# Attending two pairs of heads in one step, with both denominators in one PSUM bank and normalisation apart

## The chip, the cores and the metric

The kernel runs on one core of one Trainium2 chip. The metric is the device time of one execution in microseconds (us), as the median of the runs shown; smaller is better. The core has five engines that work side by side, each on a queue of its own that it takes in order: TensorE (PE in the profile, its weight loads PEld), VectorE (DVE), ScalarE (ACT), GpSimd (POOL) and SyncE (SP), which here only issues transfers. Matmul results stand in banks of PSUM, from which ACT and DVE move them on.

## What is computed

Three stages: linear attention with exponential features, a gated feed-forward network with an RMS norm, and a soft mixture of experts. The changed lines belong to the first stage, the features and the attention of the queries; the second stage is what runs around them.

```python
def phi(x):                                   # q, k, v: 4 x 8 heads x 576 x 64; w_phi: 64 x 128
    proj = einsum('bhsd,df->bhsf', x, w_phi)
    proj = proj - max(abs(proj), axis=-1)
    return concatenate([exp(proj), exp(-proj)], axis=-1)
q_p, k_p = phi(q), phi(k)
kv, z = einsum('bhsf,bhsd->bhfd', k_p, v), sum(k_p, axis=2)
x = einsum('bhsf,bhfd->bhsd', q_p, kv) / (einsum('bhsf,bhf->bhs', q_p, z) + 1e-6)
x = x as 2304 tokens x 512                    # then:
xn = x / sqrt(mean(x*x) + 1e-6) * rms_g
x = (silu(xn @ w_gate) * (xn @ w_val)) @ w_out          # 512 -> 1536 -> 512
return soft_moe(x)                            # 8 experts, 4 slots each, w1 and w2 per expert
```

## The kernel before

The 2304 tokens are worked in six blocks of 384. A first phase computes the features of the keys and kv for the four batches, converts the weights of the feed-forward network, and does the queries of block 0. Then the feed-forward network runs block by block, and in the background of block 0 the queries of block 1, in that of blocks 1 to 4 the queries of blocks 2 to 5 are prepared (class Reduced, the one that the change touches). Behind block 5 the experts run, for which 32 weight transfers of 1 MB are issued from block 5 on.

In a block, m runs over 12 slices of 128 hidden features. For each slice the loop writes gate(m + 1) (12 matmuls into pg, then tanh on ACT at L801 and a product on DVE at L802), value (12 matmuls into pv, a product on DVE at L806), and the output of slice m (9 matmuls into three acc banks); then t is split into hh (ACT, L102) and hl (DVE, L105), which the output matmuls of the next round read. Below, pg(m), pv(m) and acc(m) are these groups of matmuls for slice m; pg(0') is that of the next block. The products are made from high and low parts, so the inputs of a block are split too: for m = 11, split_block makes xnh0 to xnh3 (ACT) and xnl0 to xnl3 (DVE) out of xraw, the prepared queries of the next block. Each pg and pv reads them in the order xnh0, xnh0, xnl0, xnh1, and so on.

After gate, after value and after output, fill() inserts background steps: 36 slots in a block, numbered 0 to 35, slot 3m behind gate(m + 1), 3m + 1 behind its value, 3m + 2 behind the output of m. The table REDUCED says at which slot each step of the queries runs, the table PSLOTS the nine steps of post, the work on the previous block's result: three transposes at 1, 4 and 7, logits (matmuls LT) at 12, rows at 14, dturn at 16, dispatch (sps, which reads d) at 18, combine at 20, cturn (transposes ctp) at 24. The steps of the queries of one block, for 8 heads h in 4 pairs c, are:

- feature(h), L271: two matmuls into qP, a copy on ACT, an all-reduce of the largest value on POOL (L280); at slots 0, 2, 4, 8, 9, 14, 15, 20
- exps(h), L282: a subtraction on DVE and two exponentials on ACT; at slots 3, 5, 7, 11, 12, 17, 18, 23
- attend(c), L197: matmuls num (L206) and den (L214), the copy of num to xraw (ACT, L216), 1e-6 added to den (DVE, L218), reciprocal (DVE, L219), eight copies of 32 x 192 that spread it over the partitions (ACT, L224), the product with xraw (DVE, L225), a square (ACT) and the sum of squares s (DVE, L232); at slots 6, 12, 18, 24
- scale, L238: matmuls ssq over s, an inverse root in eleven steps on DVE for three values a partition, its spread to dg (DVE, L246), an all-reduce on POOL (L293); at slot 27
- out, L251: four scalings of xraw on DVE (L254); at slot 30

PSUM: three banks acc, two banks gv for pg and pv in turn, three banks misc for everything in the background. The features of a head lie in a tile e, of which there are three. The compiler's scheduler can move instructions of an engine by a few places against the order in which they are written, so that the order shown below is the one after it.

Of the kernel before, what the change touches and what calls it, by code (L numbers as in the profile page):

```python
# [7 lines left out]
F32 = mybir.dt.float32  # L8
F32R = mybir.dt.float32r
U32 = mybir.dt.uint32  # L10
AF = mybir.ActivationFunctionType
ALU = mybir.AluOpType
# [4 lines left out]
NB, NH, SEQ, HD, DF = 4, 8, 576, 64, 128  # L17
NT, DM, DFF = 2304, 512, 1536
# [3 lines left out]
BLK = 384  # L22
# [6 lines left out]
KCONV, MCONV = (3, 2), (2, 1)  # L29
# [6 lines left out]
REDUCED = [0, 0, 2, 3, 5, 6, 4, 8, 7, 11, 12, 9, 14, 12, 17, 18, 15, 20, 18, 23, 24, 27, 30]  # L36
# [28 lines left out]
def tile_kernel(ctx: ExitStack, tc: tile.TileContext, q2T, qT, kT, v, wbd, wg, wv, wo, rmsg, phi, w1, w2, consts, out):  # L65
# [107 lines left out]
    kvt = {}  # L173
# [82 lines left out]
    class Reduced(Q):  # L256
# [14 lines left out]
        def feature(self, h):  # L271
            x = self.x.pop(h)
            self.split(h + 1)
            self.load(h + 4)
            p = self.psum("qP", [128, BLK])
            PE.matmul(out=p, lhsT=ws, rhs=x, start=True, stop=False)
            PE.matmul(out=p, lhsT=wl, rhs=x, start=False, stop=True)
            e = self.e[h] = self.sp.tile([128, 2, BLK], F32, tag="e", name="qe", bufs=3)
            ACT.copy(out=e[:, 1], in_=p)  # L279
            POOL.partition_all_reduce(e[:, 0], e[:, 1], channels=128, reduce_op=bass_isa.ReduceOp.absmax)  # L280
# [6 lines left out]

        def spare(self):
            e = self.sp.tile([128, 2, BLK], F32, tag="e", name="dg", bufs=3)
            return e[:, 0], e[:, 1]  # L290
# [9 lines left out]
        def steps(self):  # L300
            def first():
                self.split(0)
                self.load(3)

            f = [lambda h=h: self.feature(h) for h in range(NH)]
            a = [lambda c=c: self.attend(c) for c in range(4)]
            g = [lambda h=h: self.exps(h) for h in range(NH)]
            s = [first, *(x for c in range(4) for x in (f[2 * c], f[2 * c + 1], g[2 * c], g[2 * c + 1], a[c])), self.scale, self.out]
            return sorted(zip(REDUCED, s), key=lambda x: x[0])

# [291 lines left out]
    Z_run = stp.tile([96, 1], F32, name="Z_run")  # L602
    with ExitStack() as p2:
# [228 lines left out]
        for _ in range(2):  # L832
            conv_load(sp, MCONV, sp, stp)
        for blk in range(NBLK):
            acc = [ps.tile([128, DM], F32, tag=f"acc{i}", name=f"acc{i}", bufs=1) for i in range(TPB)]
            qsteps, qnext = qnext or [], None
            if blk == 1:
# [7 lines left out]
                S_run = stp.tile([128, 2 * DM], F32, tag="S", name="S_run", bufs=1)[0:96, 0:DM]  # L845
# [21 lines left out]
            def fill():  # L867
                done[0] += 1
                if blk == 0:
# [6 lines left out]
                    if n == 2:  # L876
                        conv_load(sp, MCONV, sp, stp)
# [183 lines left out]
```

## Time and profile before

| what | us |
|---|---|
| median of 3 runs | 748.27 (746.10 to 750.22) |
| the profiled execution, its own time | 745.82 |
| its span, first to last instruction | 743.8 |
| TensorE busy in the span | 714.6 (96%) |
| DVE, ACT, POOL busy | 428.1, 371.2, 108.3 |

The span is what the trace covers; the time of an execution lies some 2 us above it. An engine counts as busy while one of its instructions runs; matmuls are pipelined, so their lengths in a timeline overlap, and the distance from one start to the next is what one costs. Behind a timeline row stands, in brackets, how long the engine was idle before it and which instruction it waited for. Idle time of an engine costs only if the bound engine waits for it.

### The profile page before, as it was taken

What the parts mean: (1) busy time and instruction counts of PE and PEld (TensorE: products, weight loads), DVE (VectorE), ACT (ScalarE), POOL (GpSimd) and SP (SyncE); (2) the same over time, 40 slices, a digit from 0 to 9 for tenths busy, and PEclk for the clock granted to TensorE, in tenths of its full rate; (3) what the DMA queues carried; (4) which work ended last, traced back from release to release, by engine and by line L of the source; (5) the groups of instructions that cost most, each with busy time, mean ns of one, the idle gap of its engine ahead of it and who ended that gap; (6) DMA issues with size and microseconds to landing.
All of it is one profiled execution on the core that took longest, in us unless ns stands there. A gap on an engine that the chain in (4) does not pass through costs nothing.

```text
span 743.8 us, 12360 instructions
## 1 busy us (share of the span) xinstructions
PE 714.6 (96%) x4919; PEld 576.0 (77%) x4919; DVE 428.1 (58%) x808; ACT 371.2 (50%) x805; POOL 108.3 (15%) x60
## 2 busy tenths in 40 slices
PE   6999898999899999999999999999999999999994
PEld 4555554888789888898888988889888899988343
DVE  5888956688746557555575565655556453332413
ACT  6789854688644465344653446533465331212102
POOL 0222210134200112011120121101211010000100
PEclk9999999999999999999999999999999999999997
DMA  9674211545010100101000010000100046567898
GB/s 321 231 251 171 72 44 45 200 158 200 1 61 22 33 22 22 48 0 33 22 23 20 1 33 22 23 19 0 33 1 2 9 170 248 204 227 291 292 385 312
DMA packets 25145, 79.45 MB, mean 107 GB/s; under 512 B 2688, under 2 KB 13376, under 8 KB 18688
## 3 DMA queue, kind: packets, MB, share of 16 engines
q1 hardware_dynamic: 24864, 77.79, 29.6%
q10 hardware_dynamic: 224, 0.88, 0.4%
q8 instruction: 38, 0.62, 0.4%
q14 instruction: 19, 0.16, 0.1%
HBM read 71.99 MB, written 6.67 MB: 106 GB/s over the span
## 4 chain that ended last, share of the span: by engine, by line
PE 73%; ACT 10%; DVE 6%; DMA 5%; issue 2%; POOL 1%; SPq 0%; ACTq 0%; DVEq 0%; POOLq 0%
PE pv L794 18%; PE pg L794 17%; PE acc L819 6%; PE acc L820 6%; PE acc L821 6%; PE num L206 4%; PE kacc L439 3%; DMA eu<-in_w_dram 2%; PE den L214 2%; ACT e L224 2%; PE kacc L448 2%; DVE wt L137 1%; DMA wraw<-in_wg_dram 1%; ACT wt L127 1%; PE P L394 1%
## 5 line engine op out<-in xcount | busy, mean ns | idle before, releaser
L794 PE MATMUL pv<-xnh,wv 128*128 128x384 f32 x576 | 151.5, 344 | 0.0
L794 PE MATMUL pg<-xnh,wg 128*128 128x384 f32 x576 | 150.2, 342 | 1.2 <-DVE t L802 1.0
L794 PEld LDWEIGHTS pg<-xnh,wg 128*128 128x128 f32 x576 | 104.7, 188 | 7.2 <-DVE t L802 1.5
L794 PEld LDWEIGHTS pv<-xnh,wv 128*128 128x128 f32 x576 | 103.1, 188 | 7.0 <-issue 6.7
L794 PE MATMUL pv<-xnl,wv 128*128 128x384 f32 x288 | 97.7, 339 | 0.0
L794 PE MATMUL pg<-xnl,wg 128*128 128x384 f32 x288 | 97.5, 338 | 0.0
L819 PE MATMUL acc<-wo,hh 128*128 128x512 f32 x216 | 88.5, 410 | 0.4 <-ACT hh L102 0.4
L280 POOL PARTITION_ALL_REDUCE qe<-qe x32 | 50.0, 1561 | 262.7 <-ACT qe L279 243.0
L820 PE MATMUL acc<-wo,hh 128*128 128x512 f32 x216 | 85.8, 397 | 0.0
L821 PE MATMUL acc<-wo,hl 128*128 128x512 f32 x216 | 85.3, 395 | 0.0
L102 ACT CAST hh<-t 128x384 fp32r<-128x384 f32 x72 | 36.7, 510 | 80.9 <-PE acc L820 69.8
L105 DVE TENSOR_TENSOR hl<-t,hh 128x384 fp32r<-128x384 f32 x72 | 41.3, 574 | 53.7 <-ACT hh L102 51.2
L802 DVE SCALAR_TENSOR_TENSOR t<-t,pg 128x384 f32<-128x384 f32 x72 | 39.7, 551 | 51.7 <-ACT t L801 51.6
L801 ACT ACTIVATE t<-pg 128x384 f32<-128x384 f32 x72 | 35.1, 488 | 62.8 <-PE pg L794 62.8
L224 ACT COPY qe<-qe 32x192 f32<-32x192 f32 x128 | 44.8, 350 | 31.7 <-DVE qe L219 30.4
L806 DVE TENSOR_TENSOR t<-t,pv 128x384 f32<-128x384 f32 x72 | 39.7, 552 | 30.3 <-PE pv L794 29.0
L794 PEld LDWEIGHTS pg<-xnl,wg 128*128 128x128 f32 x288 | 54.0, 188 | 0.3 <-DVE xnl L105 0.3
L794 PEld LDWEIGHTS pv<-xnl,wv 128*128 128x128 f32 x288 | 54.1, 188 | 0.1
L439 PE MATMUL kacc<-kp,vt 128*64 128x256 f32 (+1 forms) x320 | 43.9, 399 | 5.4 <-ACT kp L416 5.3
L821 PEld LDWEIGHTS acc<-wo,hl 128*128 128x128 f32 x216 | 40.6, 188 | 9.8
L819 PEld LDWEIGHTS acc<-wo,hh 128*128 128x128 f32 x216 | 40.7, 189 | 8.1 <-ACT hh L102 0.9
L820 PEld LDWEIGHTS acc<-wo,hh 128*128 128x128 f32 x216 | 40.7, 188 | 6.5
(187 smaller groups left out, 1069.3 us busy)
## 6 DMA issues: line engine op xcount, KB each, us to landing
eu<-in_w_dram SPq DMA_DIRECT2D x32, 1024.0 KB, 6.0
wraw<-in_wg_dram SPq DMA_DIRECT2D x6, 1024.0 KB, 5.3
wraw<-in_wv_dram SPq DMA_DIRECT2D x6, 1024.0 KB, 6.5
wraw<-in_wo_dram SPq DMA_DIRECT2D x6, 1024.0 KB, 6.2
qraw<-in_qT_dram SPq DMA_DIRECT2D x32, 192.0 KB, 2.3
raw<-in_kT_dram SPq DMA_DIRECT2D x18, 256.0 KB, 3.7
vt<-in_v_dram SPq DMA_DIRECT2D x18, 256.0 KB, 2.9
out_dram<-ob SPq DMA_DIRECT2D x18, 256.0 KB, 3.4
```

What stands on the lines that cost most here:

```text
L102: ACT.copy(out=hi, in_=src)
L105: (lo_eng or POOL).tensor_tensor(out=lo, in0=src, in1=hi.bitcast(F32), op=ALU.subtract)
L224: ACT.copy(out=rd[64 * hh + 32 * r:64 * hh + 32 * r + 32, g], in_=dn[o:o + 32])
L280: POOL.partition_all_reduce(e[:, 0], e[:, 1], channels=128, reduce_op=bass_isa.ReduceOp.absmax)
L439: PE.matmul(out=kva[o0:o0 + 64, hh // 2], lhsT=self.vt[r0:r1, h], rhs=kp[r0:r1, hh].rearrange("p s f -> p (s f)"), start=first and hh < 2, ...
L794: PE.matmul(out=p, lhsT=w[:, a, c], rhs=x, start=n == 0, stop=n == 11)
L801: ACT.activation(out=t, in_=g, func=AF.Tanh, scale=0.5)
L802: DVE.scalar_tensor_tensor(out=t, in0=t, scalar=1.0, in1=g, op0=ALU.add, op1=ALU.mult)
L806: DVE.tensor_tensor(out=t, in0=t, in1=wide("v", m, xs), op=ALU.mult)
L819: PE.matmul(out=acc[i], lhsT=hh[:, s], rhs=w[:, 0], start=m == 0, stop=False)
L820: PE.matmul(out=acc[i], lhsT=hh[:, s], rhs=w[:, 1], start=False, stop=False)
L821: PE.matmul(out=acc[i], lhsT=hl[:, s], rhs=w[:, 0], start=False, stop=m == MF - 1)
```

## The change

In place of attend(c) at four slots there are two steps attend2(c0), for pairs 0 and 1 at slot 12 and for pairs 2 and 3 at slot 24. Each takes num of the first pair, num of the second, then den of both, in two halves of one misc bank; so it holds all three misc banks where attend(c) held two. The evictions of num and the additions of 1e-6 belong to it. The rest, from the reciprocal to the sum of squares, is a step normalise(c) for each pair, at slots 13, 14, 25 and 26. Features and exponentials keep their slots. scale moves from 27 to 29, out from 30 to 31. Since features now wait longer for their attend, there are five tiles e. To make room, S_run (the running result of dispatch) gets a tile of its own, and the second buffer of the weight conversion in block 0 moves to the pool of the first.

```diff
--- before.py
+++ after.py
@@ -26,14 +26,14 @@
 NJ = MF // 2
 NPRE = 9
 LOW = 0.93 * 2.0 ** -29
-KCONV, MCONV = (3, 2), (2, 1)
+KCONV, MCONV = (3, 2), (2, 2)
 NX = 3
 NLEFT = 2
 ELEFT = 4
 CTURN = 4
 CEVERY = 3
 PSLOTS = [1, 4, 7, 12, 14, 16, 18, 20, 24]
-REDUCED = [0, 0, 2, 3, 5, 6, 4, 8, 7, 11, 12, 9, 14, 12, 17, 18, 15, 20, 18, 23, 24, 27, 30]
+REDUCED = [0, 0, 2, 4, 8, 9, 14, 15, 20, 3, 5, 7, 11, 12, 17, 18, 23, 12, 24, 13, 14, 25, 26, 29, 31]
 TURNED0 = [2, 8, 14, 20, 12, 15, 20, 26, 28, 31]
 TURNED1 = [0, 7, 14, 21, 6, 13, 20, 26, 28, 30]
 
@@ -275,7 +275,7 @@
             p = self.psum("qP", [128, BLK])
             PE.matmul(out=p, lhsT=ws, rhs=x, start=True, stop=False)
             PE.matmul(out=p, lhsT=wl, rhs=x, start=False, stop=True)
-            e = self.e[h] = self.sp.tile([128, 2, BLK], F32, tag="e", name="qe", bufs=3)
+            e = self.e[h] = self.sp.tile([128, 2, BLK], F32, tag="e", name="qe", bufs=5)
             ACT.copy(out=e[:, 1], in_=p)
             POOL.partition_all_reduce(e[:, 0], e[:, 1], channels=128, reduce_op=bass_isa.ReduceOp.absmax)
 
@@ -285,8 +285,57 @@
             ACT.activation(out=e[:, 0], in_=e[:, 1], func=AF.Exp)
             ACT.activation(out=e[:, 1], in_=e[:, 1], func=AF.Exp, scale=-1.0)
 
+        def attend2(self, c0):
+
+            if c0 == 0:
+                xraw[self.blk] = xp.tile([128, 4, BLK], F32, tag="xraw", name="xraw", bufs=1)
+            cs = c0, c0 + 1
+            nums = {c: self.psum("num", [128, BLK]) for c in cs}
+            for c in cs:
+                for b, t0, t1 in block_parts(self.blk):
+                    for s in range(2):
+                        for hh in range(2):
+                            PE.matmul(out=nums[c][64 * hh:64 * hh + 64, t0:t1], lhsT=kvt[b][:, 2 * c + hh, s, 0:HD],
+                                      rhs=self.e[2 * c + hh][:, s, t0:t1], start=s == 0, stop=s == 1, skip_group_check=True)
+            den = self.psum("den", [128, 2, BLK // 2])
+            for n, c in enumerate(cs):
+                for s in range(2):
+                    for hh in range(2):
+                        for g in range(2):
+                            o, t = 64 * hh + 32 * g, BLK // 2 * g
+                            b = (self.blk * BLK + t) // SEQ
+                            PE.matmul(out=den[o:o + 32, n], lhsT=kvt[b][:, 2 * c + hh, s, HD:HD + 1].to_broadcast([128, 32]),
+                                      rhs=self.e[2 * c + hh][:, s, t:t + BLK // 2], start=n == 0 and s == 0, stop=n == 1 and s == 1, skip_group_check=True)
+            for n, c in enumerate(cs):
+                ACT.copy(out=xraw[self.blk][:, c], in_=nums[c])
+                DVE.tensor_scalar(out=self.e[2 * c][:, 0, 0:BLK // 2], in0=den[:, n], scalar1=1e-6, scalar2=None, op0=ALU.add)
+            for b, t0, t1 in block_parts(self.blk):
+                if c0 == 2 and self.blk * BLK + t1 == (b + 1) * SEQ and b + 2 < NB:
+                    kvt[b + 2] = kvp.tile([128, NH, 2, HD + 1], F32, tag="kv", name=f"kv{b + 2}", bufs=2)
+                    SP.dma_start(out=kvt[b + 2].rearrange("p h s d -> p (h s d)"), in_=kv_d[b + 2])
+
+        def normalise(self, c):
+            y = xraw[self.blk][:, c]
+            e = [self.e.pop(2 * c), self.e.pop(2 * c + 1)]
+            dn = e[0][:, 0, 0:BLK // 2]
+            DVE.reciprocal(out=dn, in_=dn)
+            rd = e[1][:, 0].rearrange("p (g t) -> p g t", g=2)
+            for hh in range(2):
+                for g in range(2):
+                    o = 64 * hh + 32 * g
+                    for r in range(2):
+                        ACT.copy(out=rd[64 * hh + 32 * r:64 * hh + 32 * r + 32, g], in_=dn[o:o + 32])
+            DVE.tensor_tensor(out=y, in0=y, in1=e[1][:, 0], op=ALU.mult)
+            if c == 0:
+                self.s = self.sp.tile([128, BLK], F32, tag="s", name="s", bufs=1)
+                ACT.activation(out=self.s, in_=y, func=AF.Square)
+            else:
+                sq = e[1][:, 1]
+                ACT.activation(out=sq, in_=y, func=AF.Square)
+                DVE.tensor_tensor(out=self.s, in0=self.s, in1=sq, op=ALU.add)
+
         def spare(self):
-            e = self.sp.tile([128, 2, BLK], F32, tag="e", name="dg", bufs=3)
+            e = self.sp.tile([128, 2, BLK], F32, tag="e", name="dg", bufs=5)
             return e[:, 0], e[:, 1]
 
         def spread(self, r, dg):
@@ -303,9 +352,10 @@
                 self.load(3)
 
             f = [lambda h=h: self.feature(h) for h in range(NH)]
-            a = [lambda c=c: self.attend(c) for c in range(4)]
+            a = [lambda c=c: self.attend2(c) for c in (0, 2)]
+            d = [lambda c=c: self.normalise(c) for c in range(4)]
             g = [lambda h=h: self.exps(h) for h in range(NH)]
-            s = [first, *(x for c in range(4) for x in (f[2 * c], f[2 * c + 1], g[2 * c], g[2 * c + 1], a[c])), self.scale, self.out]
+            s = [first, *f, *g, *a, *d, self.scale, self.out]
             return sorted(zip(REDUCED, s), key=lambda x: x[0])
 
     class Turned(Q):
@@ -600,6 +650,7 @@
     stp = pool(ctx, "stp")
     nM_run = [stp.tile([96, 1], F32, name=f"nM_run{i}") for i in range(2)]
     Z_run = stp.tile([96, 1], F32, name="Z_run")
+    S_run = stp.tile([96, DM], F32, name="S_run")
     with ExitStack() as p2:
         mctx = p2.enter_context(ExitStack())
         pctx = p2.enter_context(ExitStack())
@@ -830,7 +881,7 @@
         q.begin()
         qnext = q.steps(TURNED1[0:4], TURNED1[4:8], TURNED1[8:], lag=3)
         for _ in range(2):
-            conv_load(sp, MCONV, sp, stp)
+            conv_load(sp, MCONV, sp)
         for blk in range(NBLK):
             acc = [ps.tile([128, DM], F32, tag=f"acc{i}", name=f"acc{i}", bufs=1) for i in range(TPB)]
             qsteps, qnext = qnext or [], None
@@ -842,7 +893,6 @@
                 q.begin()
                 qsteps = q.steps()
                 sp = pool(pctx, "post", side="right")
-                S_run = stp.tile([128, 2 * DM], F32, tag="S", name="S_run", bufs=1)[0:96, 0:DM]
             if blk == NBLK - 1:
                 pctx.close()
                 qctx.close()
@@ -874,7 +924,7 @@
                     else:
                         conv_join()
                     if n == 2:
-                        conv_load(sp, MCONV, sp, stp)
+                        conv_load(sp, MCONV, sp)
                 for f in plan[done[0] - 1]:
                     f()
 
```

Line numbers of the rows that follow are those of each file: L794, L806 and L821 of before are L845, L857 and L872 of the changed kernel.

First place: ACT around slot 24 in block 1, behind tanh of gate(9) (num is the matmul result that is evicted, qe the tile e).

Before:

```order
L801 ACTIVATE t<-pg 128x384
L216 COPY xraw<-num 128x384
L224 COPY qe<-qe 32x192 x8
L102 CAST hh<-t 128x384
L231 ACTIVATE qe<-xraw 128x384
L801 ACTIVATE t<-pg 128x384
```

Now:

```order
L852 ACTIVATE t<-pg 128x384
L310 COPY xraw<-num 128x384 x2
L327 COPY qe<-qe 32x192 x8
L102 CAST hh<-t 128x384
L327 COPY qe<-qe 32x192
L334 ACTIVATE qe<-xraw 128x384
L327 COPY qe<-qe 32x192 x7
L852 ACTIVATE t<-pg 128x384
L334 ACTIVATE qe<-xraw 128x384
```

A second set of eight copies and a second square stand between the cast hh and the next tanh, the last square behind that tanh.

Second place: TensorE around ssq in block 1, behind pg(10) before and behind acc(9) now.

Before:

```order
L794 MATMUL pg<-xnh_2373,wg_2091 128x384 x2
L794 MATMUL pg<-xnl_2374,wg_2091 128x384
L241 MATMUL ssq<-small,s 128x1 x3
L794 MATMUL pv<-xnh_2361,wv_2160 128x384 x2
L794 MATMUL pv<-xnl_2362,wv_2160 128x384
```

Now:

```order
L870 MATMUL acc_2423<-wo_1997,hh 128x512
L871 MATMUL acc_2423<-wo_1997,hh 128x512
L872 MATMUL acc_2423<-wo_1997,hl 128x512
L241 MATMUL ssq<-small,s 128x1 x3
L845 MATMUL pg<-xnh_2362,wg_2092 128x384 x2
L845 MATMUL pg<-xnl_2363,wg_2092 128x384
```

Before, pv(10), acc(9), pg(11), pv(11) and acc(10) stood between ssq and pg(0'); now pg(11), pv(11) and acc(10).

Third place: DVE from dg to the split of the next block, at the end of block 1 (t<-t,pg and t<-t,pv are the two products of gate(11) and value; hl belongs to slice 10 before and to slice 11 now), and TensorE there.

DVE before:

```order
L246 TENSOR_TENSOR dg_3162<-cst_72,ms_3147 128x384
L254 SCALAR_TENSOR_TENSOR xraw_2604<-xraw_2604,small_77,dg_3162 128x384
L105 TENSOR_TENSOR hl_3189<-t_3140,hh_3188 128x384
L254 SCALAR_TENSOR_TENSOR xraw_2604<-xraw_2604,small_77,dg_3162 128x384 x3
L802 SCALAR_TENSOR_TENSOR t_3211<-t_3211,pg_3198 128x384
L105 TENSOR_TENSOR xnl0_3246<-xraw_2604,xnh0_3245 128x384
L105 TENSOR_TENSOR xnl1_3250<-xraw_2604,xnh1_3249 128x384
L105 TENSOR_TENSOR xnl2_3254<-xraw_2604,xnh2_3253 128x384
L806 TENSOR_TENSOR t_3211<-t_3211,pv_3218 128x384
L105 TENSOR_TENSOR xnl3_3258<-xraw_2604,xnh3_3257 128x384
```

DVE now:

```order
L246 TENSOR_TENSOR dg_3187<-cst_72,ms_3172 128x384
L853 SCALAR_TENSOR_TENSOR t_3209<-t_3209,pg_3196 128x384
L254 SCALAR_TENSOR_TENSOR xraw_2726<-xraw_2726,small_77,dg_3187 128x384 x2
L857 TENSOR_TENSOR t_3209<-t_3209,pv_3212 128x384
L254 SCALAR_TENSOR_TENSOR xraw_2726<-xraw_2726,small_77,dg_3187 128x384 x2
L105 TENSOR_TENSOR xnl0_3244<-xraw_2726,xnh0_3243 128x384
L105 TENSOR_TENSOR xnl1_3248<-xraw_2726,xnh1_3247 128x384
L105 TENSOR_TENSOR hl_3240<-t_3209,hh_3239 128x384
L105 TENSOR_TENSOR xnl2_3252<-xraw_2726,xnh2_3251 128x384
L105 TENSOR_TENSOR xnl3_3256<-xraw_2726,xnh3_3255 128x384
```

TensorE now, from the last matmul of acc(10) (before, pg(0') ran in one piece):

```order
L872 MATMUL acc_2423<-wo_2262,hl 128x512
L845 MATMUL pg<-xnh_3243,wg_235 128x384 x2
L845 MATMUL pv<-xnh_3243,wv_364 128x384
L845 MATMUL pg<-xnl_3244,wg_235 128x384
L845 MATMUL pg<-xnh_3247,wg_235 128x384 x2
L845 MATMUL pg<-xnl_3248,wg_235 128x384
```

The product of gate(11) has moved ahead of the scalings and that of value in between them; all four scalings still stand ahead of xnl0. One matmul of pv(0') has moved in between the second and third of pg(0').

## Rows read from the trace of the kernel before

**Rows 1.** Page, part 1: busy us of each engine (share), instructions.

```profile
PE 714.6 (96%) x4919; PEld 576.0 (77%) x4919; DVE 428.1 (58%) x808; ACT 371.2 (50%) x805; POOL 108.3 (15%) x60
```

**Rows 2.** Busy by stretch: length, PE PEld DVE ACT POOL, clock, DMA share, GB/s.

```profile
239.00:332.50 93.50, 93.21 (x564) 80.92 (x563) 53.11 (x105) 45.85 (x108) 15.01 (x9) 1.00 0.09 25
```

**Rows 3.** Timeline, TensorE at slot 6: start, length, line, operation, count [idle].

```profile
253.65 0.34 PE L794 MATMUL pg<-xnl,wg 128*128 128x384 f32 x1
253.92 1.51 PE L206 MATMUL num<-qe,kv 128*64 128x384 f32 x8
255.36 0.86 PE L214 MATMUL den<-qe,kv 128*32 128x192 f32 x16
256.15 0.62 PE L794 MATMUL pv<-xnh,wv 128*128 128x384 f32 x2
256.60 0.34 PE L794 MATMUL pv<-xnl,wv 128*128 128x384 f32 x1
```

**Rows 4.** Timeline, TensorE from slot 24 of block 1 to block 2.

```profile
303.36 1.51 PE L206 MATMUL num<-qe,kv 128*64 128x384 f32 x8
304.80 0.86 PE L214 MATMUL den<-qe,kv 128*32 128x192 f32 x16
...
305.87 0.59 PE L794 MATMUL pv<-xnh,wv 128*128 128x384 f32 x2
...
312.73 0.83 PE L241 MATMUL ssq<-small,s 128*128 128x1 f32 x6 [0.29 <-DVE s L232]
313.42 0.60 PE L794 MATMUL pv<-xnh,wv 128*128 128x384 f32 x2
...
317.73 0.52 PE L794 MATMUL pg<-xnh,wg 128*128 128x384 f32 x2
...
319.85 0.52 PE L794 MATMUL pv<-xnh,wv 128*128 128x384 f32 x2
...
324.07 0.52 PE L794 MATMUL pg<-xnh,wg 128*128 128x384 f32 x2
```

**Rows 5.** Timeline, DVE, the same stretch.

```profile
305.72 0.36 DVE L218 TENSOR_SCALAR qe<-den 128x192 f32<-128x192 f32 x1 [1.18 <-PE den L214]
...
306.63 1.34 DVE L219 RECIPROCAL qe<-qe 128x192 f32<-128x192 f32 x1
...
312.12 0.56 DVE L232 TENSOR_TENSOR s<-s,qe 128x384 f32<-128x384 f32 x1
313.60 0.16 DVE L243 TENSOR_SCALAR ms<-ssq 128x3 f32<-128x3 f32 x1 [0.92 <-PE ssq L241]
...
316.68 0.56 DVE L246 TENSOR_TENSOR dg<-cst,ms 128x384 f32<-128x384 f32 x1
319.95 0.62 DVE L254 SCALAR_TENSOR_TENSOR xraw<-xraw,small,dg 128x384 f32<-128x384 f32 x1 [2.72 <-POOL dg L293]
...
320.96 1.67 DVE L254 SCALAR_TENSOR_TENSOR xraw<-xraw,small,dg 128x384 f32<-128x384 f32 x3
...
323.01 1.49 DVE L105 TENSOR_TENSOR xnl<-xraw,xnh 128x384 fp32r<-128x384 f32 x3
```

**Rows 6.** Timeline, ACT, the same stretch.

```profile
308.06 2.88 ACT L224 COPY qe<-qe 32x192 f32<-32x192 f32 x8 [2.64 <-DVE qe L219]
...
320.66 0.51 ACT L102 CAST xnh<-xraw 128x384 fp32r<-128x384 f32 x1
```

**Rows 7.** Timeline, POOL, the same stretch.

```profile
317.40 2.52 POOL L293 PARTITION_ALL_REDUCE dg<-dg  x1 [19.61 <-DVE dg L246]
```

**Rows 8.** Timeline, DVE and TensorE at slot 18 of block 1.

```profile
286.08 0.25 DVE L658 COPY d<-dtp 128x96 f32<-128x96 f32 x1
...
289.16 1.03 PE L663 MATMUL sps<-x,d 128*32 128x512 f32 x6
```

**Rows 9.** Busy by stretch in the first phase, columns as in rows 2.

```profile
113.50:116.90 3.40, 2.91 (x27) 2.33 (x28) 2.48 (x10) 2.42 (x6) 0.00 (x0) 1.00 0.45 178
116.90:120.30 3.40, 3.40 (x20) 1.57 (x20) 3.30 (x12) 1.10 (x3) 0.00 (x0) 0.50 0.10 39
```

## The prediction

> **What bounds the kernel now.** The busy times of the page come first: TensorE is busy 714.6 of 743.8 us, DVE 428.1, ACT 371.2, POOL 108.3 [rows 1]. Such a share is an average over stages, so the next view is busy time by stretch, for one of the four blocks that the change touches: from 239.0 to 332.5 us (block 1) TensorE is busy 93.21 of 93.50 us at clock 1.00, DVE 53.11, ACT 45.85 [rows 2]. Inside these blocks the time can only change if TensorE gets less to do or begins to wait. Its one wait there is seen in the timeline: ssq waits 0.29 us for DVE's sum of squares [rows 4]; there are four such waits, one in each block.
>
> Then the timelines of all engines at the end of a block, to see how far ahead of TensorE the others run. The next block's first gate, here pg(0'), starts at 324.07 [rows 4]. What it needs comes out of one chain: ssq at 312.73 on TensorE [rows 4], the inverse root in small steps on DVE from 313.60, dg at 316.68 [rows 5], POOL's all-reduce from 317.40 for 2.52 us [rows 7], the scaling of xraw on DVE from 319.95 [rows 5], the xnh casts on ACT from 320.66 [rows 6], the xnl differences on DVE from 323.01 [rows 5]. The first xnh is there at 321.17, 2.9 us ahead of pg(0'); the first xnl at about 323.55, 0.9 us ahead of the third matmul, which reads it. So the chain is hidden, with less than 1 us to spare at its tightest place.
>
> **TensorE's own work.** The matmuls of attend are the same in number, shape and kind; four pairs per block before and after. What goes is a trip: the pair at slot 6 stood alone between wide matmuls. There pg's last matmul starts at 253.65; twelve take 2.12 us (317.73 to 319.85 [rows 4]), 0.18 each, so num could start at 253.83 and starts at 253.92; after den, pv's first two take 0.45 us (256.15 to 256.60) where two usually take 0.35 [rows 3]. That is 0.09 + 0.10, and up to 0.1 more in the last rows of den. I take 0.3 per block (0.2 to 0.4): -1.2 us in four blocks. The other pairs lie beside LT and ctp, narrow matmuls that cause the trip in any case; at slot 18 sps now makes it alone.
>
> The Trainium skill says it too, on its page TensorEngine Tiling (Array Packing), under Key Properties: a change of tiling mode, not merely of the tile, drains the TensorE. The trace agrees, with the 0.09 and 0.10 us. Going by that rule one would also count the lost change from 64 to 32 columns at slot 18, four changes in a block instead of three, and the gain would be 1.6 us and not 1.2.
>
> **The end of the block, where the sum is made.** The second double attend stands at slot 24, where one pair stood. I keep the clock of rows 4 and let its num start at 303.36. The second pair adds a num (1.44, 303.36 to 304.80) and a den (at most 0.79, 255.36 to 256.15 [rows 3]): 2.23 us. pv(9) then starts not at 305.87 but at 308.10. From there to ssq it was 6.86 us less 0.29 of waiting = 6.57; now a pv and an acc stand ahead of ssq too, 4.31 (313.42 to 317.73 [rows 4]) less 0.09 for the trip. TensorE reaches ssq at 308.10 + 6.57 + 4.22 = 318.89.
>
> Is the sum of squares there by then? Both denominators are added to, one after the other (0.36 more), so the first reciprocal starts at 306.63 + 2.23 + 0.36 = 309.22 [rows 5] and ends at 310.56. ACT's eight copies follow, 2.88 [rows 6]: 313.52. Behind them ACT has a cast hh and a square, some 0.51 each like the cast in [rows 6], and the second pair's eight copies: 317.42. DVE has the second reciprocal ready by 312.5, so ACT does not wait for it. From the last copy to the finished sum it was 1.74 (310.94 to 312.68 [rows 5, 6]): 319.16. So ssq waits 0.27 where it waited 0.29: no change, and it starts at 319.16.
>
> Now the distance that matters: scale has moved from slot 27 to 29, out from 30 to 31, while the split of the next block stays. Behind ssq TensorE had pv, acc, pg, pv, acc, 11.34 us to pg(0') (312.73 to 324.07 [rows 4]). It now has pg, pv, acc: 0.69 + 4.31 + 2.12 = 7.12 us. The chain does not get shorter with it: from ssq to the first scaling it was 319.95 - 312.73 = 7.22 [rows 4, 5]. In the small steps one large DVE operation stands where two did, which saves about 0.4: 6.8. Then 0.71 to the cast and 0.51 for it: the first xnh is there 8.0 us behind ssq, 0.9 too late. With it TensorE can do three matmuls (two of pg, one of pv that the order puts there), 0.53: 8.55. The next needs the first xnl. DVE's order puts two scalings, the product of gate and value, two more scalings and only then this xnl; they follow each other by 0.5 to 0.56 us (three in 1.67, three in 1.49 [rows 5]): 5 x 0.53 + 0.55 = 3.2 behind 6.8, that is 10.0, and 1.45 us of waiting. After that an xnl comes every 0.5 us and TensorE needs one every 0.53. Together 2.35; I take 2.3 us per block: +9.2 us. Ends: 1.5 us, with a chain of 6.5 and DVE's steps at 0.47; 3.0 with 7.2 and one more wait for the third xnl, which stands behind hl. Nothing takes it back: TensorE is the bound in the next block too, and the weight loads of the last stages are issued from block 5's own steps.
>
> **The middle of the block.** At slot 12 two pairs stand instead of one; ACT gets one more eviction, eight more copies and a square (0.5 + 2.88 + 0.5 us), DVE a reciprocal. Behind them wait tanh of the gate, the casts hh, and the features' copies. The nearest thing for which TensorE could wait is d for sps: d was done 2.83 us ahead (286.33 against 289.16 [rows 8]); the pair between them, 2.23, is gone, which leaves 0.6. Of the 3.9 us more on ACT, 2.2 lie beside the second pair's own matmuls; of the other 1.7 about half falls into ACT's idle time, so that d comes some 0.9 later: 0.3 us of waiting, 0 to 1.1. Four blocks: +1.2.
>
> **Costed at nothing.** Two more e buffers remove waits that TensorE never saw; S_run's own tile and the second weight buffer of the conversion leave the order of all engines as it was up to block 1; SP's and POOL's orders do not change at all. The double attend holds all three misc banks, so LT and ctp now wait for num's eviction; that copy (about 0.5 us) runs while 2.23 us of matmuls stand between, and if that cover failed it would cost its 0.5.
>
> **The sum.** Per block 2.3 - 0.3 + 0.3 + 0.0 = +2.3; four blocks +9.2 us. The profiled execution took 745.82 us, its span 743.8: 755.0. The median of the runs, 748.27, is 2.45 above the profiled one; on it the sum gives **757.5**. With all lower ends, and ssq's wait gone: 4 x (1.5 - 0.4 - 0.27) = +3.3, 751.6. With all upper ends: 4 x (3.0 - 0.2 + 1.1) = +15.6, 763.9.
>
> **Rivals.** *The clock falls at the block ends.* In 113.5 to 116.9 us TensorE had small matmuls, was busy 2.91 of 3.40 us, and for the next 3.40 us the granted clock was 0.50, the lower level [rows 9]. Waits of 0.9 and 1.45 us close together could do that. Each time costs up to 1.7 us; in all four blocks 4 x 1.7 = 6.8: 764.3. Against it: in the blocks as they are the clock stays at 1.00 [rows 2], and only 2.3 of 93 us would be idle. *Not slower: the end of the chain stays hidden.* Place: the first xnl against the third matmul of pg(0'). It decides from the point at which that xnl is ready 7.65 us behind ssq; my rows say 10.0. For it: spans on POOL are rough, and 2.52 us of the chain are POOL's. Against it: DVE's scaling waited 2.72 us for exactly that step [rows 5], alike in four blocks. Then only the trips count, and the waits of ssq go with an earlier sum: -1.2 - 1.1 = -2.3, 746.0. *The middle piles up.* If all 3.9 us of ACT's added work came late to d, sps would wait 3.9 - 0.6 = 3.3 and not 0.3: 4 x 3.0 more, 769.5. Against it: ACT is busy 45.85 of 93.5 us [rows 2].
>
> **How the numbers follow.** My forecast has 0.72, the clock 0.15, hidden 0.08, pile-up 0.05. Predicted is 757.5. From 750 to 765 lie the forecast with both its ends and the clock's case; hidden and pile-up are left out, 0.13, with a little of the edges. A measurement of this kernel can tell about 0.5% (3.7 us) from no change. Hidden, at 746.0, lies within that; so does the lowest edge of the forecast: same 0.12. Faster needs more than the hidden case gives: 0.03. Slower 0.85.
>
> **What would show it.** Right: among TensorE's waits, pg waiting for xnh or xnl, four times near 1 us each; ssq about 7 us ahead of the next block's first pg; DVE idle 2.7 us ahead of its first scaling with the product of gate and value behind it; busy TensorE time lower by about 1 us while the span grows. A wait of sps for d shows the middle term. Wrong: no wait of pg at the block's end (chain mis-sized), clock below 1.00 in a stretch of blocks 1 to 4 (the clock's case), or long waits at sps, acc or pv in the middle.

## The result and the profile after

| | before | changed |
|---|---|---|
| median of four runs, us | 747.54 (746.10 to 750.22) | 757.46 (755.01 to 758.18) |
| profiled execution, us | 745.82 | 758.18 |
| its span, us | 743.8 | 756.3 |

Three of the four runs of before are those behind the median of 748.27 that the forecast started from. The changed kernel is slower: ratio 1.0118, 95% interval 1.0094 to 1.0142, which is 7.0 to 10.6 us; the medians lie 9.9 us apart. The forecast was 757.5. The sum behind it has terms that are off in both directions and nearly cancel; the runs below take them apart.

The page, part 1 (as [rows 1]), and the waits of TensorE at the end of the blocks (engine, line, waited for: us in total, times, longest):

```profile
PE 721.3 (95%) x4919; PEld 582.7 (77%) x4919; DVE 423.7 (56%) x808; ACT 370.2 (49%) x805; POOL 108.5 (14%) x60
```

```profile
PE pg L845 <- DVE xnl L105: 4.4, 4, 1.1
PE pg L845 <- ACT xnh L102: 3.6, 5, 0.8
```

TensorE has the same 4919 instructions and is busy 6.7 us more, not 1 us less as forecast; and pg waits for xnl and xnh, which it hardly did before. Now the timelines of the changed kernel that answer to [rows 4, 5, 6, 7], at the end of block 1: TensorE, DVE, ACT, POOL (start, length, engine, line, operation, count, idle before).

```profile
299.98 2.80 PE L298 MATMUL num<-qe,kv 128*64 128x384 f32 x16
302.71 1.51 PE L307 MATMUL den<-qe,kv 128*32 128x192 f32 x32
304.15 0.53 PE L739 MATMUL ctp<-cst,c 128*96 128x128 f32 x3
...
315.25 0.80 PE L241 MATMUL ssq<-small,s 128*128 128x1 f32 x6
...
322.11 0.40 PE L872 MATMUL acc<-wo,hl 128*128 128x512 f32 x1
323.34 0.62 PE L845 MATMUL pg<-xnh,wg 128*128 128x384 f32 x2 [0.83 <-ACT xnh L102]
323.80 0.38 PE L845 MATMUL pv<-xnh,wv 128*128 128x384 f32 x1
325.26 0.44 PE L845 MATMUL pg<-xnl,wg 128*128 128x384 f32 x1 [1.09 <-DVE xnl L105]
...
328.14 0.52 PE L845 MATMUL pg<-xnl,wg 128*128 128x384 f32 x1
```

```profile
314.54 0.56 DVE L335 TENSOR_TENSOR s<-s,qe 128x384 f32<-128x384 f32 x1
...
318.79 0.56 DVE L246 TENSOR_TENSOR dg<-cst,ms 128x384 f32<-128x384 f32 x1
...
322.07 1.15 DVE L254 SCALAR_TENSOR_TENSOR xraw<-xraw,small,dg 128x384 f32<-128x384 f32 x2 [2.25 <-POOL dg L342]
323.13 0.55 DVE L857 TENSOR_TENSOR t<-t,pv 128x384 f32<-128x384 f32 x1
323.60 1.14 DVE L254 SCALAR_TENSOR_TENSOR xraw<-xraw,small,dg 128x384 f32<-128x384 f32 x2
324.66 1.02 DVE L105 TENSOR_TENSOR xnl<-xraw,xnh 128x384 fp32r<-128x384 f32 x2
```

```profile
322.78 1.04 ACT L102 CAST xnh<-xraw 128x384 fp32r<-128x384 f32 x2 [3.97 <-DVE xraw L254]
```

```profile
319.52 2.52 POOL L342 PARTITION_ALL_REDUCE dg<-dg  x1 [25.78 <-DVE dg L246]
```

The last group of acc is issued by 322.34 (322.11 and the 0.23 us from one of its matmuls to the next), and only at 323.34 does the next block's first pg start, when the first xnh is there; then two of pg, one of pv, and again a wait, until DVE has made the first xnl. Later in the same stretch single matmuls take 0.52 (the row at 328.14) where they took 0.34. The busy times by stretch (columns as in [rows 2]) say why:

```profile
326.30:329.70 3.40, 3.40 (x12) 3.40 (x11) 1.26 (x3) 0.49 (x1) 0.00 (x0) 0.50 0.00 0
515.30:518.70 3.40, 1.48 (x7) 1.06 (x7) 3.40 (x8) 2.36 (x5) 0.00 (x0) 1.00 0.00 0
518.70:522.10 3.40, 3.40 (x21) 3.35 (x20) 1.80 (x4) 0.49 (x1) 0.00 (x0) 1.00 0.00 0
```

Behind the waits at the end of block 1 the granted clock is 0.50 for 3.4 us, the 1.2 GHz level, with 12 matmul records in the stretch; such stretches also raise TensorE's busy time, since the same matmuls last longer in them. At the end of block 3 TensorE waits as long (busy 1.48 of 3.40 us), and the clock stays at 1.00 then and behind it, with 21 records. The clock's records show such falls at the ends of blocks 1, 2 and 4 of this execution.

What a block costs is read best from one ssq to the next, since ssq stands at the same place in each block. Here the starts of ssq in the changed kernel:

```profile
315.25 0.80 PE L241 MATMUL ssq<-small,s 128*128 128x1 f32 x6
...
411.66 0.58 PE L241 MATMUL ssq<-small,s 128*128 128x1 f32 x4
...
508.12 0.80 PE L241 MATMUL ssq<-small,s 128*128 128x1 f32 x6
...
602.99 0.80 PE L241 MATMUL ssq<-small,s 128*128 128x1 f32 x6
```

That is 96.41, 96.46 and 94.87 us; the first two periods hold a fall of the clock, the third holds none. So a fall costs 1.5 us here. Before, the three periods are 93.35, 93.37 and 93.33. Without a fall the change costs 1.5 us a block, and with one 3.1.

### The profile page after: what moved, and what is told of

Read it like the earlier page. It is cut to its first block, busy times and chain, and to the rows that moved or that the text cites. A ratio compares the mean times of both kernels' runs of the same rounds, so it can differ in the third digit from the quotient of the medians.

```text
span 756.3 us, 12319 instructions
## 1 busy us (share of the span) xinstructions
PE 721.3 (95%) x4919; PEld 582.7 (77%) x4919; DVE 423.7 (56%) x808; ACT 370.2 (49%) x805; POOL 108.5 (14%) x60
## 4 chain that ended last, share of the span: by engine, by line
PE 70%; ACT 9%; DVE 9%; DMA 5%; issue 3%; POOL 3%; SPq 0%; POOLq 0%; DVEq 0%; ACTq 0%
PE pg L845 17%; PE pv L845 17%; PE acc L871 6%; PE acc L870 6%; PE acc L872 6%; PE num L298 3%; DMA eu<-in_w_dram 2%; PE kacc L489 2%; ACT e L224 2%; PE den L307 2%; PE kacc L498 1%; DVE wt L137 1%; DMA wraw<-in_wg_dram 1%; ACT wt L127 1%; POOL dg L342 1%
## 5 line engine op out<-in xcount | busy, mean ns | idle before, releaser
L845 PE MATMUL pg<-xnh,wg 128*128 128x384 f32 x576 | 153.2, 347 | 4.5 <-ACT xnh L102 3.6
L845 PE MATMUL pv<-xnh,wv 128*128 128x384 f32 x576 | 152.6, 345 | 0.0
L845 PEld LDWEIGHTS pg<-xnh,wg 128*128 128x128 f32 x576 | 106.1, 191 | 11.5 <-ACT xnh L102 5.7
L845 PEld LDWEIGHTS pv<-xnh,wv 128*128 128x128 f32 x576 | 104.7, 189 | 6.2 <-issue 4.7
L845 PE MATMUL pg<-xnl,wg 128*128 128x384 f32 x288 | 99.4, 345 | 4.4 <-DVE xnl L105 4.4
L845 PE MATMUL pv<-xnl,wv 128*128 128x384 f32 x288 | 98.5, 342 | 0.0
L872 PE MATMUL acc<-wo,hl 128*128 128x512 f32 x216 | 85.4, 395 | 0.0
L845 PEld LDWEIGHTS pg<-xnl,wg 128*128 128x128 f32 x288 | 55.1, 191 | 5.7 <-DVE xnl L105 5.7
L845 PEld LDWEIGHTS pv<-xnl,wv 128*128 128x128 f32 x288 | 54.6, 190 | 0.1
L857 DVE TENSOR_TENSOR t<-t,pv 128x384 f32<-128x384 f32 x72 | 39.6, 550 | 23.4 <-PE pv L845 22.1
L872 PEld LDWEIGHTS acc<-wo,hl 128*128 128x128 f32 x216 | 40.6, 188 | 9.8
```

The source lines that it names most:

```text
L845: PE.matmul(out=p, lhsT=w[:, a, c], rhs=x, start=n == 0, stop=n == 11)
L857: DVE.tensor_tensor(out=t, in0=t, in1=wide("v", m, xs), op=ALU.mult)
L872: PE.matmul(out=acc[i], lhsT=hl[:, s], rhs=w[:, 0], start=False, stop=m == MF - 1)
```

## The experiments

The theory that came out of this: the late place of scale and out makes the waits at the end of a block, the waits bring falls of the clock, and the double attend itself is a gain. The rivals: the doubled work on ACT makes the waits; the double attend costs time by itself; the clock's falls have other causes. Periods are from ssq to ssq in blocks 1 to 4, as above.

**The end alone.** The kernel before with two numbers changed:

```diff
-REDUCED = [..., 18, 23, 24, 27, 30]
+REDUCED = [..., 18, 23, 24, 29, 31]
```

> The kernel before with nothing but its last two slots changed: scale 27 to 29, out 30 to 31; the pairs stay at 6, 12, 18, 24, one at a time. Theory (the place of scale and out makes the waits): per block pg(0') waits near 1.0 us for xnh and near 1.3 us for xnl, some 2.4 us with the restarts, ssq waits no longer (-0.29): +2.1 a block, +8.5 us, and up to 1.5 us more in every block where the clock falls behind these waits: ratio 1.010 to 1.019. Rival (ACT's doubled copies at slot 24 delay the chain): no wait of pg at the block's end, ratio 0.998.

Measured: 756.18 against 747.91 us, ratio 1.0106 (1.0076 to 1.0136). TensorE's waits:

```profile
PE pg L794 <- DVE xnl L105: 4.4, 4, 1.1
PE pg L794 <- ACT xnh L102: 3.6, 5, 0.8
```

The same waits to a tenth of a microsecond, with one pair at a time and ACT's work undoubled: the rival falls. The periods are 96.80, 95.32 and 95.26, with one fall, at 325.9 us, in the first. Without a fall that is 0.40 us a block more than the 94.89 of the changed kernel (the mean of its four such periods, three of them in further executions below): with the late end in both, the pairing makes a block shorter.

**The pairing without the late end.** The changed kernel, with its second half earlier:

```diff
-REDUCED = [0, 0, 2, 4, 8, 9, 14, 15, 20, 3, 5, 7, 11, 12, 17, 18, 23, 12, 24, 13, 14, 25, 26, 29, 31]
+REDUCED = [0, 0, 2, 4, 8, 9, 14, 15, 17, 3, 5, 7, 11, 12, 17, 18, 20, 12, 21, 13, 14, 22, 23, 27, 30]
```

> The changed kernel with its second half earlier: feature 7 at 17 (20), exps 7 at 20 (23), the second double attend at 21 (24), normalise at 22 and 23 (25, 26), scale at 27 and out at 30 as in the kernel before. Theory: ssq lies 11 us ahead of pg(0') again, so no wait of pg at the block's end, no fall of the clock in blocks 1 to 4, and ssq does not wait for the sum either; the double attend at 21 and ctp at 24 make separate trips, which takes back most of what the pairing gains: 0.3 to 0.6 us a block less than before, ratio 0.997 to 0.999. Rival (attending two pairs at once costs time by itself, by a pile-up on ACT and DVE behind it): waits of TensorE in the middle of the block, ratio 1.003 or more.

Measured: 744.06 us, ratio 0.9946 (0.9927 to 0.9965), faster than the kernel before, and by more than expected. Busy time by stretch over the four blocks:

```profile
239.00:612.00 373.00, 373.00 (x2302) 330.90 (x2301) 207.78 (x424) 183.33 (x435) 60.74 (x36) 1.00 0.09 28
```

TensorE is busy throughout, at clock 1.00. The periods are 92.19, 92.23 and 92.18: 1.15 us less a block than before. So the pairing costs nothing in waits here, and the 94.89 of the changed kernel are 92.20 and 2.69 us for the late end.

**One pair at a time, ended earlier**, to part the gain of the pairing from that of ssq's missing wait. The kernel before with

```diff
-REDUCED = [0, 0, 2, 3, 5, 6, 4, 8, 7, 11, 12, 9, 14, 12, 17, 18, 15, 20, 18, 23, 24, 27, 30]
+REDUCED = [0, 0, 2, 3, 5, 6, 4, 8, 7, 11, 12, 9, 14, 12, 17, 18, 15, 18, 18, 21, 22, 27, 30]
```

> The kernel before, one pair at a time as it was, with its last steps earlier: feature 7 at 18 (20), exps 7 at 21 (23), the last attend at 22 (24); scale and out stay at 27 and 30. Theory (e2_earlier gains by the missing wait of ssq, 0.29 us a block, and by the pairing for the rest): only the wait of ssq goes, the period of a block 93.0 us, ratio 0.998 to 0.999. Rival (all of the gain is the earlier end, the pairing gives nothing): ratio 0.995, as e2_earlier.

Measured: 745.88 us, ratio 0.9984 (0.9962 to 1.0005), periods 93.15, 93.18 and 93.15. ssq waits no longer; a block is 0.19 us shorter than before and 0.96 longer than in e2_earlier. Neither number is the price of one thing alone, because this kernel has a cost of its own: with feature 7 at slot 18, the wide qP stands between den and sps.

```profile
290.90 0.86 PE L214 MATMUL den<-qe,kv 128*32 128x192 f32 x16
291.69 0.44 PE L276 MATMUL qP<-qx,ws 128*128 128x384 f32 x1
...
292.23 1.06 PE L663 MATMUL sps<-x,d 128*32 128x512 f32 x6
```

Before, sps came straight behind den (for sps see [rows 8]):

```profile
288.49 0.86 PE L214 MATMUL den<-qe,kv 128*32 128x192 f32 x16
```

From den to sps it is 1.33 us here and was 0.67; the two qP matmuls take 0.36 of that elsewhere, so 0.3 us is the cost of their place. About 0.65 of the 0.96 is left for the pairing, and the end of ssq's wait is worth more than 0.19.

**The order inside the double attend.** e2_earlier with the matmuls in the old order and a bank for each den (each pair's evictions then follow its den):

```diff
-            nums = {c: self.psum("num", [128, BLK]) for c in cs}
-            for c in cs:
-                ...                                  # num of c
-            den = self.psum("den", [128, 2, BLK // 2])
-            for n, c in enumerate(cs):
-                ...                                  # den[:, n] of c
+            for c in cs:
+                nums[c] = self.psum("num", [128, BLK])
+                ...                                  # num of c
+                dens[c] = self.psum("den", [128, BLK // 2])
+                ...                                  # den of c
```

> The kernel of the earlier second half (e2_earlier) with the matmuls of the double attend in the old order, num, den, num, den, and each den in a bank of its own; four misc tiles then pass through three banks. Theory (the pairing gains by fewer changes between wide, 64-column and 32-column matmuls): two more changes a double attend, 0.1 to 0.2 us each, four doubles of eight: 0.4 to 0.7 us a block more than e2_earlier, ratio 0.997 to 0.998 against before. Rival (the gain of e2_earlier is the missing wait of ssq alone): as e2_earlier, 0.9946. A second rival (the shared bank frees a bank that was needed): waits of TensorE for an eviction, above 0.998.

Measured: 745.29 us (the median of ten executions, of which one took 3918.31 us and the others 743.63 to 748.71), ratio 0.9962 (0.9943 to 0.9982), periods 92.77, 92.79 and 92.78: 0.58 us a block more than e2_earlier. The timeline of TensorE at slot 21 of block 1:

```profile
294.94 1.51 PE L299 MATMUL num<-qe,kv 128*64 128x384 f32 x8
296.38 0.86 PE L307 MATMUL den<-qe,kv 128*32 128x192 f32 x16
297.16 1.51 PE L299 MATMUL num<-qe,kv 128*64 128x384 f32 x8
298.61 0.86 PE L307 MATMUL den<-qe,kv 128*32 128x192 f32 x16
299.39 0.62 PE L844 MATMUL pv<-xnh,wv 128*128 128x384 f32 x2
```

num and den come one after the other without a wait: no bank is missing. The same stretch of e2_earlier:

```profile
295.62 2.80 PE L298 MATMUL num<-qe,kv 128*64 128x384 f32 x16
298.35 1.51 PE L307 MATMUL den<-qe,kv 128*32 128x192 f32 x32
299.78 0.62 PE L845 MATMUL pv<-xnh,wv 128*128 128x384 f32 x2
```

4.45 us from the first num to pv against 4.16, which is 0.29 for one double attend and 0.58 for the two of a block: by estimate, about 0.15 us for each of the four changes between the forms that a block has more. So of the 0.96 us a block between e6_single_early and e2_earlier, 0.58 come from num, num, den, den; the other 0.38 come from two places instead of four and from qP's place in e6_single_early, which this run does not part. The interval of the ratio overlaps that of e2_earlier; the reading rests on the periods, which repeat to 0.04 us.

**A shorter chain with the late end.** The changed kernel with the spread of the inverse root on TensorE:

```diff
-            POOL.partition_all_reduce(r, dg, channels=128, reduce_op=bass_isa.ReduceOp.add)
+            r = self.psum("r", [128, BLK])
+            PE.matmul(out=r, lhsT=ones_sb[:, 0:1].to_broadcast([128, 128]), rhs=dg, start=True, stop=True)
```

> The changed kernel with its slots as they are, but the chain shorter: the spread of the inverse root is a matmul with ones on TensorE, as in block 1's queries, in place of POOL's all-reduce of 2.52 us. Theory (the length of the chain behind ssq makes the waits): the first scaling comes 2 us sooner behind ssq, no wait of pg of more than 0.2 us, no fall of the clock; the added matmul costs 0.9 to 1.3 us a block with its trip: 0.0 to 0.4 us a block against before, ratio 0.999 to 1.003. Rival (the waits come from elsewhere): waits of pg stay, ratio 1.015 or more.

Measured: 748.26 us, ratio 1.0001 (0.9984 to 1.0019), periods 93.42, 93.48 and 93.44, no fall of the clock in blocks 1 to 4. DVE's first scaling now starts 5.17 us behind ssq (322.69 against 317.52) instead of 6.82, and pg waits no more at a block's end; the new matmul waits for dg, in total:

```profile
PE r L343 <- DVE dg L246: 0.6, 4, 0.2
```

So it is the length of the chain against the distance from ssq to pg(0'), as the theory has it. A block is 1.2 us longer than in e2_earlier: 1.0 of it lies around the new matmul (1.39 us from the pv matmul ahead of it, at 321.27, to the second one behind it, at 322.66, where two steps of pv take 0.36), and 0.2 at ssq, which is held up as in the changed kernel (below).

**A filled wait.** The changed kernel with five wide matmuls ahead of pg(0') whose result nobody reads:

```diff
+NFILL = 5
...
+                    if blk:
+                        pz = post_tile("fillP", [128, BLK])
+                        for z in range(NFILL):
+                            PE.matmul(out=pz, lhsT=W["g", 0][:, 0, 0:128], rhs=W["g", 0][:, 0, 128:128 + BLK], start=z == 0, stop=z == NFILL - 1)
                     xs = split_block(xraw.pop(blk + 1))
```

> The changed kernel with five wide matmuls added ahead of pg(0') in blocks 1 to 4, on weights that are in SBUF anyway; nothing reads their result. They take 0.9 us, about the wait of pg for xnh. Theory (the granted clock falls because two waits follow each other closely): the wait for xnh is filled, so the added work costs at most 0.3 us a block, the wait for xnl of 1.3 us stays, the clock falls in none or one of the four blocks instead of three: ratio 1.006 to 1.010. Rival (the clock's fall is not tied to the waits): clock below full in as many blocks as in the changed kernel, ratio 1.012 to 1.015.

Measured: 756.62 us, ratio 1.0105 (1.0069 to 1.0141), just outside what was expected. The first wait is filled: pg waits for xnl alone, longer than in the changed kernel, and the periods are 95.40, 95.43 and 95.40, with no fall of the clock in any of the four blocks.

```profile
PE pg L846 <- DVE xnl L106: 5.2, 4, 1.3
```

A block costs 0.5 us more than one of the changed kernel without a fall, not 0.3 at most; four times that is 2.1 us, more than one fall costs.

**Which blocks the clock falls in.** Four further executions. The changed kernel twice:

> The changed kernel again, to see in which blocks the granted clock falls. Theory (each pair of waits at a block's end can bring one fall of 3.4 us, not each does): the same waits of 0.83 and 1.09 us in all four blocks, a fall behind one to four of them and nowhere else in blocks 1 to 4; a block with a fall lasts 96.4 us, one without 94.9. Rival (the falls have a fixed place in the program): the same three blocks as in the first profile.

> The changed kernel a third time. Theory: a fall behind one to four pairs of waits, in other blocks than in the run before it; periods of 94.9 us without, 96.4 us with. Rival: the same blocks each time.

Measured: 762.11 and 755.36 us. r1_changed has falls behind the waits of blocks 1, 2 and 4, the same three as in the first profile (periods 96.43, 96.36 and 94.89); r2_changed behind those of block 3 alone, with the same waits (0.85 and 1.08 in block 1) in all four. The stretches of r2_changed behind the four ends:

```profile
326.30:329.70 3.40, 3.40 (x19) 3.34 (x20) 2.28 (x5) 0.84 (x2) 0.00 (x0) 1.00 0.00 0
421.20:424.60 3.40, 3.40 (x20) 3.35 (x20) 2.28 (x5) 0.81 (x2) 0.00 (x0) 1.00 0.00 0
516.00:519.40 3.40, 3.35 (x10) 3.35 (x11) 1.87 (x4) 0.43 (x2) 0.00 (x0) 0.51 0.00 0
612.50:615.90 3.40, 3.40 (x19) 3.35 (x20) 2.28 (x5) 0.83 (x2) 0.00 (x0) 1.00 0.27 43
```

Its periods are 94.88, 94.91 and 96.41. The falls have no fixed place in the program, so the rival is out.

> The kernel of e1_tail_only again. Theory: as in the changed kernel, a fall behind one to four of its pairs of waits, in other blocks than block 1 alone; 95.3 us for a block without, 96.8 with. Rival: again block 1 alone.

Measured: 754.97 us, and no fall at all behind the four pairs of waits, periods 95.27, 95.33 and 95.26. At least one had been expected.

> The kernel of e3_fill again. Theory (a filled first wait takes away the fall of the clock): no fall in blocks 1 to 4, all periods 95.4 us. Rival (its first profile was chance): one fall or more.

Measured: 757.32 us, no fall, periods 95.42, 95.45 and 95.41; clock over the four blocks:

```profile
239.00:612.00 373.00, 368.85 (x2262) 323.16 (x2261) 202.32 (x413) 177.93 (x426) 60.02 (x36) 1.00 0.07 21
```

Together: 8 falls at the 20 pairs of waits of the two kernels with the late end (7 of 12 in the changed one, 1 of 8 in e1_tail_only), each of them starting between 0.3 us ahead of the end of the second wait and 1.0 us behind it. The six kernels without these waits (before, e2_earlier, e4_pe_spread, e5_two_banks, e6_single_early, e7_cturn21) have none at their 24 block ends, in one profile each. So the falls belong to the waits. None came at the 8 filled pairs either, but that does not show that the filling prevents them: the 8 are only two executions, and r4_tail has none at its four unfilled pairs. Why some pairs bring a fall and others of the same length do not stays open, and also whether the changed kernel has more of them than e1_tail_only by more than chance.

**ctp beside the second double attend.** e2_earlier with

```diff
-PSLOTS = [1, 4, 7, 12, 14, 16, 18, 20, 24]
+PSLOTS = [1, 4, 7, 12, 14, 16, 18, 18, 21]
```

> e2_earlier with combine at slot 18 (20) and cturn at 21 (24), so that ctp follows den of the second double attend and makes no trip of its own. Theory (a trip costs 0.2 to 0.3 us): 1 us less in four blocks, ratio 0.993 to 0.994. Rival (combine's chain on DVE is not done by then, or holds up the products): waits of TensorE for the transposes' input or for a gv bank, ratio 0.996 or more.

Measured: 744.25 us, ratio 0.9943 (0.9922 to 0.9964), periods 92.14, 92.18 and 92.14. That is 0.05 us a block, not 0.25: the trip of ctp alone costs next to nothing. As a kernel it is no different from e2_earlier; both beat the kernel before and the changed one.

## Why the prediction was right, and where its steps were off

Per block, forecast against what the rows of before and of the changed kernel show (the starts of its matmuls, in blocks without a fall):

| step | forecast, us | measured, us | from |
|---|---|---|---|
| TensorE's own work | -0.3 | -0.65 | num and den 8.67 to 8.22; the trip at slot 6, 0.19 |
| wait of ssq | 0.0 | -0.3 | held up by 0.55 before, by 0.23 now |
| middle of the block | +0.3 | 0 | no wait in the changed kernel |
| end of the block | +2.3 | +2.5 | two waits, 2.28, and two restarts, 0.2 |
| clock | a rival, 4 x 1.7 in all | 1.5 for each fall | 94.9 to 96.4 |

The steps add up to the 1.54 us between the periods, 93.35 and 94.89. The same 1.54 in runs, before to e6_single_early to e2_earlier to the changed kernel, are -0.19, -0.96 and +2.69; these are not the terms one by one, since e6_single_early has a cost of its own, and since the late end also brings back part of ssq's wait, which e2_earlier has not.

**The end of the block was right**, mechanism and size. The first scaling starts 6.82 us behind ssq (forecast 6.8), the first xnh is ready some 8.0 behind it (322.78 + 0.51 - 315.25; forecast 8.0), and the matmul that needs the first xnl starts 10.0 behind it (325.26; forecast for the xnl 10.0). The waits from start to start are 1.00 (322.34 to 323.34) and 1.28 (323.98 to 325.26), 2.28 together against 2.35; each restart, not priced in the forecast, adds about 0.1, since the first two matmuls take 0.46 instead of 0.35 and the first behind the second wait 0.28 instead of 0.18.

**The term for TensorE's own work was half of what came.** At slot 12 of block 1, before and then now:

```profile
270.15 1.51 PE L206 MATMUL num<-qe,kv 128*64 128x384 f32 x8
271.59 0.86 PE L214 MATMUL den<-qe,kv 128*32 128x192 f32 x16
272.26 1.05 PE L632 MATMUL LT<-x2T,phi_sb 128*32 128x128 f32 x24
```

```profile
266.93 2.80 PE L298 MATMUL num<-qe,kv 128*64 128x384 f32 x16
...
270.98 1.05 PE L683 MATMUL LT<-x2T,phi_sb 128*32 128x128 f32 x24
```

From num to what follows den, the four pairs took 2.23, 2.11, 2.11 and 2.22 us before (slots 6, 12, 18 and 24); the two double attends take 4.05 and 4.17 (299.98 to 304.15 in the rows above). The trip at slot 6 was priced right: 0.09 ahead of num, 0.10 in pv, and a den that takes 0.79 in front of pv where it takes 0.67 in front of LT, 0.31 in all. The step that failed left the rest as it was: it let the second pair cost a whole num and den, 2.23 us, and it costs 1.94 and 1.95. Two nums in a row take 2.73 where two single ones take 2.88, since the change from num to den, too, is paid once instead of twice, 0.15 us each time (e5_two_banks). The rule that the prediction set beside it, a drain at every change of tiling mode (the Trainium skill, TensorEngine Tiling (Array Packing), Key Properties), gave 1.6 us in place of 1.2 and so pointed the right way; the rows have 2.6.

**ssq's wait** was forecast to stay, 0.27 us where it was 0.29. Most of it went. The matmul ahead of ssq, before and now:

```profile
312.11 0.33 PE L794 MATMUL pg<-xnl,wg 128*128 128x384 f32 x1
```

```profile
314.86 0.40 PE L872 MATMUL acc<-wo,hl 128*128 128x512 f32 x1
```

Before, ssq started 0.62 us behind it, where such a pg takes 0.18, and its six matmuls took 0.69, where they take 0.58 in e2_earlier: held up by 0.55. Now it starts 0.39 behind it, where such an acc takes 0.23, and the six take 0.66: 0.23. The sum is finished at 315.10 and ssq starts at 315.25, earlier than forecast, since the second pair is shorter than priced and DVE's two additions take 0.62 together and not 0.72.

**The middle** was put at 0.3 us and came out at zero, though the reading behind it holds. d is ready 0.14 us ahead of sps, where it was 2.83 ahead in [rows 8]:

```profile
285.37 0.25 DVE L709 COPY d<-dtp 128x96 f32<-128x96 f32 x1
...
285.76 1.06 PE L714 MATMUL sps<-x,d 128*32 128x512 f32 x6
```

So the cover was used up almost to the last, and not overdrawn.

**The sum.** Without the clock a block costs -0.65 - 0.3 + 2.5 = 1.5 us more, four of them 6.2. The other 3.7 of the 9.9 us are as much as 2.4 falls of 1.5 us would cost; the three profiles of the changed kernel show 3, 3 and 1 in these blocks. That the falls are all of it is not shown: the interval of the difference is 3.6 us wide, and what lies behind block 4 varies as well (from its ssq to the end of the span it is 151.0 us before and 154.4 in e6_single_early, with the same work there). The fall of the clock, set beside the forecast as a rival with 0.15 and listed as a sign that the forecast is wrong, is part of what happened, in some blocks of each profiled execution of the changed kernel. Forecast 757.5 and measured 757.46 agree because some 0.95 us a block that was gained or not lost, and not forecast, stands against 0.2 us at the end and up to 0.9 of clock, not forecast either; the median of before, too, came out 0.7 us lower than the one that the forecast started from. The direction, the place and the size of the wait were read from the rows; the last microseconds are luck.

The rivals that ended elsewhere: the hidden end is ruled out by the waits at the block's end, the pile-up by the absence of waits in the middle.

## What to carry to other kernels

Where a chain through several engines feeds the next block, measure it from the instruction of the bound engine that starts it to the one that needs its result, and compare that with the work of the bound engine in between: moving the start two slots later took 4.2 us of cover from a chain that had less than 1 us to spare, and cost 2.5 us a block, nearly four times the 0.65 that the pairing gained on TensorE. A change that bundles a gain (fewer changes of form on the bound engine) with such a move should be tried with the steps ahead of the chain moved forward too: the same double attend, ended earlier, is 0.5% faster than the kernel before.

## What the runs showed of the hardware

Two waits of TensorE close together, of 0.83 and 1.09 us with three matmuls between them, came in 8 of 20 cases with 3.4 us at a granted clock of 0.50, at a price of 1.5 us; at the 24 block ends without such waits there was no fall. With the first of the two filled by matmuls whose result nobody reads there was none in 8 cases of two executions either, though the second wait was then 1.3 us long; whether the filling did it is not shown. A change between matmuls of 64 and of 32 columns costs TensorE about 0.15 us here, by the 4.45 us of e5_two_banks against the 4.16 of e2_earlier, with two changes more. And three transposes moved from between wide matmuls to behind narrow ones saved only 0.05 us a block (e7_cturn21 against e2_earlier).
